# Cutting streamed weight loads by rows: 128 rows as one transfer, as 120+8, as 108+20 and as 63+63+2

## The chip, the cores and the metric

The kernel runs on one core of a Trainium2 chip. The metric is the device time of one execution in microseconds (us). Beside plain timed runs there is one profiled execution, whose trace holds every instruction, the semaphore updates and every DMA packet (queue, start, duration, size, but not the DMA engine that carried it). TensorE is PE here (PEld is its weight load), VectorE is DVE, ScalarE is ACT, GpSimd is POOL and SyncE is SP; a small q behind a name means the engine's instruction queue.

## The reference

Two attention mixers read the same 2048 x 640 input and are blended by a gate. Mixer A is what matters here: it goes through 64 segments of 32 tokens one after the other, because each segment hands 8 memory rows to the next.

```python
for s in range(n_seg):                       # 64 segments of 32 tokens
    xs = x[:, s * seg_len:(s + 1) * seg_len, :].copy()
    h = jnp.concatenate([mem, xs], axis=1)   # 8 memory rows + 32 tokens
    q = jnp.einsum('btd,dhe->bhte', h, Wq)   # 640 -> 32 heads x 192
    k = jnp.einsum('btd,dhe->bhte', h, Wk)
    v = jnp.einsum('btd,dhe->bhte', h, Wv)
    ...                                      # masked softmax attention over the 40 rows
    o = jnp.einsum('bhte,hed->btd', o, Wo)   # back to 640
    mem = o[:, :M, :].copy()
    outs.append(o[:, M:, :])
...
return g * a + (1 - g) * b                   # g = sigmoid(x . gate_w), b = local dilated attention
```

## The kernel before, in words

**Three stages.** Mixer B and the gate come first (`part_b`), then a pass over the last 8 tokens of all segments (`prepass`), then the loop over the 64 segments (`part_a`), and a short last stage (`part_z`). In the profiled execution the loop fills the time from about 360 to 1672 us.

**Weights.** The four weight matrices of mixer A are cut into 80 slices. A slice is 128 rows (partitions) of 3072 bytes, 384 KB. Most slices stay in SBUF for the whole loop. Fourteen of them (`N_STREAM`) do not fit and are fetched again from device memory in every segment. The list comes out of a small plan of due times in `weights_setup` (lines 510 to 534), which spreads the fourteen over the segment: seven for queries and keys, four for values, three for the output projection. The last three are read from a packed copy in device memory (`wscr`), the other eleven from the weight matrices themselves.

**The stream.** `get_slice` (line 576) gives a resident tile, or calls `load_slice`, which takes the next of five buffers (`WBUFS`, pool `wstream`, tiles `wst`) and issues one DMA from SP's queue (line 557 for the packed copy, line 558 for the matrices). SP's queue runs in order. A load can be issued as soon as PE has finished with the slice that was five places earlier in the stream, so it runs about five slices ahead of PE.

**Order of the work.** PE, ACT and DVE follow an order written out by hand in `part_a` (lines 907 to 986): projections `m_qk` (line 734), transposes `t_qk` (line 751), scores `s_a` and `s_b` (lines 781, 790), values `m_v` (line 827), the output projection `o_group` (line 891), and the selection `sel` (line 901) that makes the next segment's memory rows. ACT issues six small DMAs of its own in each segment: the result `out_dram` (line 1001), `Vz` (line 715), the next segment's tokens `hT` (line 650), a part of mixer B's result (line 954), `oz_dram` (line 968) and the next packed keys and queries `ZB` (line 710). They stand in ACT's order between its copies and exponentials.

**DMA semaphores.** All DMAs of SP and ACT share eight completion semaphores, taken in turn. In the trace each DMA waits, before it is issued, until the transfer that last used its semaphore has landed.

Of the kernel before, what the change touches and what calls it, by code (L numbers as in the profile page):

```python
# [27 lines left out]
class _K:  # L28
# [481 lines left out]
    def weights_setup(self):  # L510
        nc, tc = self.nc, self.tc
        keys = self.slice_keys()
        gap = {("q", 0, 0): 300, ("k", 0, 1): 160, ("k", 0, 3): 70, ("k", 1, 0): 450, ("k", 2, 0): 850, ("k", 3, 0): 1050,
               ("v", 1, 0): 1000, ("v", 2, 0): 600, ("v", 3, 0): 570, ("v", 3, 3): 200, ("oa", 6): 1200}
        at, t = {}, 0
        for k in keys:
            t += gap.get(k, 0)
            at[k] = t
            t += 163
        self.stream_keys = set()  # L520
        for i in range(N_STREAM):
            left = [k for k in keys if k not in self.stream_keys]
            self.stream_keys.add(min(left, key=lambda k: abs(at[k] - (i + 0.5) * t / N_STREAM)))
        rest = [k for k in keys if k not in self.stream_keys]
        use = [(m, R) for m in "qkv" for R in range(4)]
        rest.sort(key=lambda k: use.index(k[:2]) if k[:2] in use else 99)
        n = (0, N_EARLY, -N_MID - N_V - N_LAST, -N_V - N_LAST, -N_LAST, None)
        self.early, *self.late = [rest[n[x]:n[x + 1]] for x in range(5)]
        self.wres = self.ctx.enter_context(tc.tile_pool(name="wres", bufs=1))
        self.res_tiles = {}  # L530
        self.wscr = {}
        self.ahead = {}
        self.after = mybir.DependencyInfo(mybir.DependencyClass.Sync, mybir.DependencyReason.DATA)
        self.wstream = self.ctx.enter_context(tc.tile_pool(name="wstream", bufs=WBUFS))

# [13 lines left out]
    def load_slice(self, pool, key, name, tag=None, t=None):  # L549
        src = self.slice_info(key)[0]  # L550
        if t is None:
            t = pool.tile([128, 1536], BF, name=name, **({"tag": tag} if tag else {}))
            self.load_slice(pool, key, name, tag, t)
            return self.slice_view(key, t)
        v = self.slice_view(key, t)
        if key in self.wscr:
            return self.nc.sync.dma_start(t[:], self.wscr[key])
        return self.nc.sync.dma_start(v[:], src)

    def slice_view(self, key, t):  # L560
        split = self.slice_info(key)[1]
# [122 lines left out]
    def part_a(self):  # L684
# [4 lines left out]
        with ctx:  # L689
# [30 lines left out]

            sched = ctx.enter_context(tc.manual_schedule(engines={mybir.EngineType.PE, mybir.EngineType.Activation, mybir.EngineType.DVE}))
            for s in range(nseg):
                pqs, sts, pTs, pSs = {}, {}, {}, {}

                def m_qk(i, kcs):
# [391 lines left out]
```

## Time and profile before

| | before |
|---|---|
| median of two timed runs | 1725.18 us (1721.58 to 1728.78) |
| profiled execution, its own time | 1731.97 us |
| profiled execution, span from first to last instruction | 1729.2 us |
| PE busy | 1636.4 us, 95% of the span |
| DMA bytes over the span | 477.46 MB, mean 276 GB/s |
| streamed loads `wst` issued by SP | 260 + 260 + 195 + 192 of 384 KB |
| granted TensorE clock, mean | 0.990 |

PE's busy time is an upper bound of its useful time, since matmuls overlap in the pipeline and their ends are modelled. The mean share of the DMA engines adds up the durations of packets, and a packet that waits on its engine behind another queue's packet is counted too, so that the share can go above 1.

### The profile page before, as it was taken

The numbers are of one execution on the slowest core, as the hardware profiler recorded it, in microseconds if no ns is written. First come the engines' busy times: TensorE is split into PE (matmuls) and PEld (weight loads), VectorE is DVE, ScalarE is ACT, GpSimd is POOL, SyncE is SP. The second block draws the span as 40 slices with busy tenths as digits, with TensorE's granted clock in tenths as the row PEclk, the third lists the DMA queues.
The fourth block names the chain that finished last, engine by engine and source line by source line (L and its number), as shares of the span: only waits on it lengthen the run. The fifth ranks groups of instructions, "written<-read, shape, count | busy, mean of one in ns | idle before, by whom it ended". The sixth has DMA issues, their size and how long they took to land.

```text
span 1729.2 us, 82024 instructions
## 1 busy us (share of the span) xinstructions
PE 1636.4 (95%) x36281; PEld 976.2 (56%) x36281; DVE 632.3 (37%) x2031; ACT 861.4 (50%) x2338; POOL 59.8 (3%) x124
## 2 busy tenths in 40 slices
PE   7887999899999999999999999999999999999989
PEld 4544544355555655555555555556555556555667
DVE  3665333233333333333333333333333333333330
ACT  3887322235555555555555455555555545555550
POOL 2030000000000000000000000000000000000000
PEclk9999899999999999999999999999999999999999
DMA  7898695989999999899888889989899999998991
GB/s 198 202 228 199 226 319 146 273 276 298 294 301 301 299 299 308 294 294 305 298 291 298 281 290 302 301 292 306 299 297 301 297 290 303 305 300 298 310 295 31
DMA packets 299696, 477.46 MB, mean 276 GB/s; under 512 B 100172, under 2 KB 176460, under 8 KB 299340
## 3 DMA queue, kind: packets, MB, share of 16 engines
q1 hardware_dynamic: 200208, 415.76, 74.2%
q10 hardware_dynamic: 99132, 56.46, 11.5%
q8 instruction: 283, 4.64, 1.1%
q14 instruction: 73, 0.60, 0.1%
HBM read 430.40 MB, written 44.48 MB: 275 GB/s over the span
## 4 chain that ended last, share of the span: by engine, by line
PE 85%; DMA 6%; ACT 3%; issue 3%; DVE 1%; ACTq 1%; SPq 1%; DVEq 0%
PE ps_qk L734 25%; PE ps_v L827 13%; PE ps_wo L891 12%; PE ps_pre L603 6%; PE ps_qkT L751 6%; PE ps_S L781 5%; PE ps_oT L850 3%; PE ps_z L1048 3%; PE ps_pre L617 3%; ACT ZB L975 2%; DMA bqkT<-bqk_dram 2%; PE ps_bqk L234 2%; PE ps_mem L901 1%; PE ps_S L790 1%; DMA OT<-bo_dram 1%
## 5 line engine op out<-in xcount | busy, mean ns | idle before, releaser
L743 ACT CAST TZ<-ps_qk 128x384 bf16<-128x384 f32 x448 | 208.3, 479 | 333.5 <-PE ps_qk L734 189.3
L734 PEld LDWEIGHTS <-hT 128*32 128x32 bf16 x10240 | 247.0, 96 | 158.7 <-issue 17.2
L758 DVE COPY ZB<-ps_qkT 128x384 bf16<-128x384 bf16 x256 | 91.6, 358 | 376.8 <-PE ps_qkT L751 210.5
L734 PE MATMUL ps_qk<-wres_q,hT 128*32 128x384 bf16 x4096 | 225.2, 327 | 2.1 <-issue 2.1
L827 PE MATMUL ps_v<-wlate_v,hT 128*32 128x384 bf16 x4096 | 224.0, 328 | 0.0
L734 PE MATMUL ps_qk<-wlate_k,hT 128*32 128x384 bf16 x3328 | 202.7, 328 | 1.8 <-issue 1.8
L891 PEld LDWEIGHTS <-TZ 128*32 128x32 bf16 x6144 | 154.8, 96 | 68.6 <-issue 20.2
L734 PE MATMUL ps_qk<-wst,hT 128*32 128x384 bf16 x1792 | 154.0, 328 | 1.8 <-issue 1.1
L827 PEld LDWEIGHTS <-hT 128*32 128x32 bf16 x5120 | 113.4, 96 | 67.1 <-issue 4.3
L891 PE MATMUL ps_wo<-wlate_oa,TZ 128*32 128x384 bf16 x2560 | 140.1, 327 | 2.9 <-issue 2.2
L781 PE MATMUL ps_S<-ZB,TZ 128*128 128x160 bf16 (+1 forms) x1024 | 136.4, 237 | 0.3 <-DMA ZB<-zpk_dram 0.3
L891 PE MATMUL ps_wo<-wlate_ob,TZ 128*32 128x256 bf16 x2688 | 124.0, 275 | 8.4 <-issue 7.2
L751 PE MATMUL ps_qkT<-ident,TZ 128*128 128x128 bf16 x1536 | 129.7, 220 | 0.4 <-ACT TZ L743 0.3
L751 PEld LDWEIGHTS <-TZ 128*128 128x128 bf16 x1536 | 89.0, 98 | 61.2 <-issue 40.6
L799 ACT ACTIVATE ZB<-ps_S 32x224 bf16<-32x224 f32 x256 | 89.0, 348 | 42.6 <-PE ps_S L790 38.6
L861 DVE CAST TZ<-ps_oT 128x192 bf16<-128x192 f32 x256 | 79.5, 351 | 63.7 <-PE ps_oT L855 63.5
L861 ACT CAST TZ<-ps_oT 128x192 bf16<-128x192 f32 x256 | 69.8, 327 | 58.3 <-PE ps_oT L855 58.3
L781 PEld LDWEIGHTS <-TZ 128*128 128x128 bf16 (+1 forms) x1024 | 58.8, 95 | 67.8 <-issue 40.4
L904 DVE CAST hT<-ps_mem 128x24 bf16<-128x24 f32 x126 | 22.5, 179 | 202.3 <-PE ps_mem L901 202.3
L834 ACT CAST TZ<-ps_v 128x384 bf16<-128x384 f32 x192 | 92.4, 481 | 3.2
L827 PE MATMUL ps_v<-wst,hT 128*32 128x384 bf16 x1024 | 86.7, 329 | 3.6 <-DMA wst<-in_A_Wv_dram 3.6
L799 ACT ACTIVATE TZ<-ps_S 32x224 bf16<-32x224 f32 x256 | 88.8, 347 | 2.3
(137 smaller groups left out, 2229.9 us busy)
## 6 DMA issues: line engine op xcount, KB each, us to landing
wst<-in_A_Wq_dram SPq DMA_DIRECT2D x260, 384.0 KB
wst<-in_A_Wv_dram SPq DMA_DIRECT2D x260, 384.0 KB
wst<-in_A_Wk_dram SPq DMA_DIRECT2D x195, 384.0 KB
wst<-wscr SPq DMA_DIRECT2D x192, 384.0 KB
zpk_dram<-ZS ACTq DMA_DIRECT2D x4, 3072.0 KB
ZB<-zpk_dram ACTq DMA_DIRECT2D x64, 192.0 KB
wres_q<-in_A_Wq_dram SPq DMA_DIRECT2D x16, 384.0 KB
wlate_v<-in_A_Wv_dram SPq DMA_DIRECT2D x16, 384.0 KB
```

The source lines that it names most:

```text
L603: nc.tensor.matmul(ps[:], lhsT=sls[r][kc][:, c0:c0 + 128], rhs=zTi[:, kc, :], start=(kc == 0), stop=(kc == KC - 1))
L617: mm = nc.tensor.matmul(pss[g][:], lhsT=zTi[:, kc, 128 * st:128 * st + 128], rhs=sls[kc][:, 512 * g:512 * g + 512], start=(kc == 0), stop= ...
L734: nc.tensor.matmul(pq[32 * j:32 * j + 32, 0:384], lhsT=hT[:, kc, :], rhs=sl[:, 384 * j:384 * j + 384], start=(kc == 0), stop=(kc == KC - 1 ...
L743: cp(sts[i], pqs[i][:, 0:384])
L751: nc.tensor.transpose(pT[:, t, :, :, :].rearrange("p j b i -> p (j b i)"), st[:, 128 * t:128 * t + 128], self.ident[:])
L758: nc.vector.tensor_copy(q_blocks(R)[:, 1:5, :, :].rearrange("p b c i -> p c b i"), pT.rearrange("p t j b i -> p (t j) b i"))
L781: nc.tensor.matmul(grid(h, par)[:, :, 0:80].rearrange("p j (b r i) -> p j b r i", r=2, i=8)[:, :, :, r, :], lhsT=KT[k0:k1, 12 * r + c:12 * ...
L799: nc.scalar.activation(E[ps], pSs[h][ps, :, 112 * j:112 * j + 112], ACT.Exp, scale=scale_a)
L827: nc.tensor.matmul(pvs[R][32 * j:32 * j + 32, 0:384], lhsT=hT[:, kc, :], rhs=sl[:, 384 * j:384 * j + 384], start=(kc == 0), stop=(kc == KC ...
L834: cp(V[R], pvs[R][:, 0:384])
L861: cps[j % 2](oTxs[2 * h + j // 2][:, 6 * (j % 2):6 * (j % 2) + 6, :], pos[j][:, 0:240].rearrange("p (c q) -> p c q", q=40)[:, :, 8:40])
L891: nc.tensor.matmul(pso[part][32 * jj:32 * jj + 32, 0:n], lhsT=oTxs[2 * (R // 2) + j // 2][:, 6 * (j % 2) + 3 * (R % 2) + t, :], rhs=o_weig ...
```

## The change

A streamed slice is no longer always one DMA of 128 rows. A tuple `self.rows` lists row ranges, and `load_slice` issues one DMA from SP's queue for each range, into the same tile. The loop sets the tuple at the start of each segment: segments 0 to 9 and 58 to 63 keep one range of 128 rows; segments 10 to 25 use 120 and 8 rows; 26 to 41 use 108 and 20; 42 to 57 use 63, 63 and 2. The bytes are the same, and so are the buffers, the order of use and all arithmetic.

```diff
@@ weights_setup
         self.ahead = {}
+        self.rows = ((0, 128),)
         self.after = mybir.DependencyInfo(mybir.DependencyClass.Sync, mybir.DependencyReason.DATA)
@@ load_slice
         v = self.slice_view(key, t)
-        if key in self.wscr:
-            return self.nc.sync.dma_start(t[:], self.wscr[key])
-        return self.nc.sync.dma_start(v[:], src)
+        dst, src = (t, self.wscr[key]) if key in self.wscr else (v, src)
+        for r0, r1 in self.rows:
+            dma = self.nc.sync.dma_start(dst[r0:r1], src[r0:r1])
+        return dma
@@ part_a
             for s in range(nseg):
+                self.rows = (((0, 120), (120, 128)) if 10 <= s < 26 else ((0, 108), (108, 128)) if 26 <= s < 42 else
+                             ((0, 63), (63, 126), (126, 128)) if 42 <= s < 58 else ((0, 128),))
                 pqs, sts, pTs, pSs = {}, {}, {}, {}
```

## The prediction

> **What bounds the kernel now.** I read the page first (busy shares, the 40 slices, the DMA queues), then the stretches of the three groups of segments, who waited there, and last the trace's DMA packets and landings.
>
> ```profile
> PE   7887999899999999999999999999999999999989
> ...
> DMA  7898695989999999899888889989899999998991
> ...
> q1 hardware_dynamic: 200208, 415.76, 74.2%
> q10 hardware_dynamic: 99132, 56.46, 11.5%
> ```
>
> PE is at nine tenths through the loop, and so are the DMA engines: SP's queue (q1, nearly all of it the weight stream) and ACT's queue (q10) share them.
>
> ```profile
> 565.10:891.50 326.40, 315.94 (x7888) 192.12 (x7888) 116.82 (x432) 169.49 (x513) 8.11 (x16) 1.00 0.91 299
> 891.50:1220.40 328.90, 316.37 (x7883) 191.56 (x7884) 117.06 (x432) 169.48 (x512) 8.11 (x16) 1.00 0.90 296
> 1220.40:1546.20 325.80, 317.57 (x7893) 191.54 (x7892) 116.72 (x432) 169.46 (x512) 8.11 (x16) 1.00 0.91 299
> ```
>
> The columns are start and end, length, PE, PEld, DVE, ACT and POOL busy time, clock, DMA share and GB/s. The borders are the ends of the L975 copy, one per segment, so the lines are segments 10 to 25, 26 to 41 and 42 to 57. A segment takes 20.40, 20.56 and 20.36 us (length over 16), 19.70 at best; PE is busy 19.8 of it.
>
> ```profile
> PE ps_wo L891 <- issue: 7.3, 14, 1.1
> PE ps_qk L734 <- issue: 7.0, 8, 1.4
> PE ps_oT L850 <- issue: 3.5, 7, 0.9
> ```
>
> These are PE's longest waits in those 981 us. None is for a streamed slice: PE is the bound, and the stream keeps up. By how much is read from the packets. From 400 to 1640 us the trace has 108,758 stream packets of 3072 bytes, one per row: median 121 ns, mean 146.5. A load lands 4.4 to 4.7 us (median) after its issue; its buffer is needed 6.2 to 7.6 us after it. The slack is about two microseconds.
>
> **How many DMA engines a transfer uses.** The trace shows it by its landings. A 128-row load leaves 16 semaphore events, one per engine. The loads and stores of 20 rows in mixer B leave 11 (10 engines and one more from the queue itself, at once), the 8-row stores 9, the two small transfers of line 954 and line 1001, whose outer dimension is 4, leave 5. The largest divisor of the row count up to 16 fits all of these. It gives 15 engines for 120 rows, 12 for 108, 9 for 63 and 2 for 2.
>
> ```profile
> L250 SPq DMA_DIRECT2D bqkT<-bqk_dram x40: 273/358/1122, 24.3 to 169.4; - x40
> ```
>
> ```profile
> 168.40:171.00 2.60, 2.54 (x39) 1.15 (x32) 1.44 (x3) 2.15 (x4) 0.00 (x0) 0.52 0.54 105
> ```
>
> The first line are the 20-row loads (duration of the issue, min/median/max). Four are issued back to back into one tile, with no wait between them, so parts of one tile don't wait for each other. The second line is a stretch in which eight of them were in flight: a share of 0.54, under 10/16. In another, 28 to 29 us, 8 to 12 of their packets run at a time. So consecutive ones use the same ten engines and the others stand idle. I take it that every transfer begins at the same first engine.
>
> **The sum.** In rows per slice the busiest engine then carries 8 when whole, 8+1 = 9 with 120+8, 9+2 = 11 with 108+20, and 7+7+1 = 15 with 63+63+2. Fourteen slices make 112, 126, 154 and 210 packets per segment.
>
> That engine has other work in each segment. If the transfers on four engines lie on the same first ones, it is 2 x 32 packets of 320 bytes at 20 ns, 8 more for hT, 8 of 1536 bytes at 65, 16 of 768 at 36, and 20 completion packets at 9: 2.7 us, and 2.85 (two parts) or 3.0 (three) with the added completions. At the clean 121 ns the whole loads need 112 x 0.121 + 2.7 = 16.3 of 20.4 us, so the room is 4 us.
>
> What a packet costs in the parts no row shows directly. Below it can't be less than 121 ns, the undisturbed packet. Above, the nearest rows are mixer B's 20-row loads, whose 996-byte packets have medians of 69 to 92 ns in crowded stretches against 46 undisturbed, and the 3072-byte packets beside them 171 to 214 against 121: at most twice. The middle of that is 1.5 times, 181 ns. I take 146.5 ns, the mean in today's stream, because the 120-, 108- and 63-row parts are nearer to a whole load than to 20 rows.
>
> - 120+8: 126 x 0.1465 + 2.85 = 21.3 us, against 20.4: 0.9 more, over 16 segments **14 us**. (At 121: 18.1, nothing. At 181: 25.7, 84 us.)
> - 108+20: 154 x 0.1465 + 2.85 = 25.4, against 20.56: 4.85 more, **78 us**. (At 121: 15 us. At 181: 163.)
> - 63+63+2: 210 x 0.1465 + 3.0 = 33.8, against 20.36: 13.4 more, **214 us**. (At 121: 128. At 181: 330.)
>
> Together 306 us. Against the profiled execution's 1732 us (span 1729, three more around it) that is 2038; its time is 0.4% above the median of the runs, so **2030** is what I give. The ends are 1732 + 143 = 1875 and 1732 + 577 = 2309.
>
> [...]
>
> **Costs put at nothing.** The change adds 14 x 16 + 14 x 16 + 28 x 16 = 896 issues on SP at 0.33 us (the wst issues' median), 4.6 or 9.2 us per segment. They lie in SP's idle time: in these 981 us SP waited some 760 for PE.
>
> ```profile
> SPq L558 <- PE ps_qk L734: 256.2, 232, 3.0
> SPq L558 <- PE ps_wo L891: 132.2, 129, 2.4
> SPq L558 <- PE ps_v L827: 116.2, 96, 1.6
> ```
>
> Without that cover it is 42 issues x 0.37 = 15.5 us per segment in the third group, still under 20.4.
>
> The eight semaphores are the added wait. Twenty DMAs per segment become 34 and 48, and each waits for the eighth before it. Eight DMAs are then 3.3 or 2.3 slices instead of 5.6: the queue is at most that far ahead, which uses up the two microseconds of slack and brings nothing further where an engine is the bound anyway. Behind a waiting SP instruction stand only later slices. ACT is touched too: L1001 and L715 stand before the L743 copies, L954 before the exponential L799, L968 and L710 before the copies L975 and L983 on which PE's L901 and the next segment wait. Where SP lags, ACT's turn comes before its semaphore is free, and PE loses there, while the loads go on into free buffers. So I add nothing for it; it is one reason for staying above the clean ends.
>
> **Rivals.**
> [...]
> 2. *Clean packets.* Only the row counts decide, at 121 ns: 1875. For it: the median is 121 today, and part of the mean 146.5 is a packet's wait for ACT's queue, already in the 2.7 us. Against: a full queue never ran that clean.
> 3. *The eight semaphores alone.* Engines don't fill up, and a transfer lands 4.55 us after issue whatever its rows. Then a segment needs 34 x 4.55/8 = 19.3 us, nothing, or 48 x 4.55/8 = 27.3, 6.9 more: 1732 + 111 = 1843. Against: it leaves out the engines' load.
> 4. *Not slower.* The first engine changes from transfer to transfer, so the rows even out: 8 per engine on average, and a 63-row part lands sooner than a whole load (7 packets for 8). The 16.3 us stay 16.3 and the slack covers the rest: about 1732, within 25 us. It decides from the point where the busiest engine has under 20.4 us of work. Against: the ten packets at a time of the 20-row loads.
>
> **Chances.** My forecast 0.43; rival 1 0.22; rival 2 0.20; rival 3 0.06; rival 4 0.07; the rest, 0.02, is above all of these. The range 1860 to 2260 leaves out rivals 3 and 4 and the outer edges of the others, about 0.2. About 2% is what a measurement of this kernel can tell from no change. Slower by more: 0.93. Within it: 0.05, rival 4. Faster: 0.02, its lucky edge.
>
> **What would show it.** Cut at the L975 ends, segments 10 to 25 should take about 21 us, 26 to 41 about 25, 42 to 57 about 34, and the others 20.4. The DMA share should fall in this order while PE starts to wait for `DMA wst`. Landings per part should be 16 (15 and one), 9, 13, 11, 10, 10 and 3. [...] Landing counts other than these, or no waits of PE for `wst`, would make the whole argument wrong.

## The result, and the profile after

The changed kernel takes **2190.93 us** (median of two runs, 2185.70 to 2196.16) against 1725.18: 1.27 times as long, 95% interval 1.2527 to 1.2873. The profiled execution took 2185.7 us with a span of 2183.9, 454.7 more than before.

The page of the changed kernel: busy tenths and granted clock in 40 slices, then the DMA queues (packets, megabytes, share of 16 engines).

```profile
PE   8889999999887788778777877777767776777999
...
PEclk9998999999999999999989999998898888888999
DMA  7896888999888888887777777765555555556992
...
q1 hardware_dynamic: 204016, 415.78, 63.3%
q10 hardware_dynamic: 99132, 56.46, 9.9%
```

PE, at nine tenths through the whole loop before, is at seven to eight over the three groups and lowest in the last, where only half of the DMA engines' time is used. The bytes are the same; q1 has 3,808 packets more. These are completions: one per engine, 16 for a whole slice, and 15 + 8, 12 + 10 and 9 + 9 + 2 for the three cuts, so 224 x (7 + 6 + 4) = 3,808 more, to the packet. Now the three groups by themselves (start and end, length, PE, PEld, DVE, ACT, POOL busy, clock, DMA share, GB/s):

```profile
562.40:999.30 436.90, 349.49 (x7876) 195.00 (x7876) 117.59 (x432) 171.66 (x512) 8.15 (x16) 0.96 0.87 221
999.30:1441.20 441.90, 350.19 (x7888) 190.94 (x7888) 117.66 (x432) 171.52 (x512) 8.15 (x16) 0.97 0.73 220
1441.20:1998.10 556.90, 394.57 (x7896) 208.28 (x7898) 118.52 (x432) 172.66 (x513) 8.15 (x16) 0.87 0.54 176
```

Over 16 segments these are 27.3, 27.6 and 34.8 us per segment: 110, 113 and 231 us more than the same segments took before, 454 in all, which is the difference of the spans. What lies outside the groups moved by less than 3 us on either side.

PE's longest waits over the three groups (line, releaser: us in total, times, longest):

```profile
PE ps_qk L738 <- DMA wst<-in_A_Wq_dram: 99.2, 127, 3.8
PE ps_wo L895 <- DMA wst<-wscr: 86.7, 87, 3.0
PE ps_qk L738 <- DMA wst<-in_A_Wk_dram: 73.2, 92, 3.0
PE ps_v L831 <- DMA wst<-in_A_Wv_dram: 58.2, 81, 2.0
```

In these four lines PE waits 317 us for streamed slices; before, none of its longest waits was for one. Its own busy time grew too, by 144 us (1094 against 950) with the same matmuls. The two together are 461 us, about the difference. The granted clock, 1.00 before, was 0.96, 0.97 and 0.87. By itself that would make the busy time 4, 3 and 15% longer; it grew by 11, 11 and 24%, and what makes up the rest is open. A busy time that grows in this way is no sign that PE is the bound: the stretch with the most waiting has the lowest clock.

The first group differs from the other two in one more way: its DMA share is nearly that of before (0.87 against 0.91), and yet it moves 221 GB/s where 299 were moved. Its engines are hardly more idle; their packets take longer (188 ns for a weight packet on average, against 146.5). SP's queue in the first group:

```profile
SPq L559 <- DMA oz_dram<-TZ: 48.7, 13, 6.2
SPq L559 <- DMA wst<-in_A_Wv_dram: 44.4, 43, 2.0
SPq L559 <- DMA hT<-xh_dram: 43.5, 16, 4.4
SPq L559 <- DMA out_dram<-ZB: 28.8, 14, 3.5
SPq L559 <- DMA wst<-in_A_Wq_dram: 27.8, 21, 2.3
```

It used to wait for PE to free a buffer. Now it waits for landings, and three of these five are transfers that ACT issued: nothing but the shared completion semaphores ties them to SP.

### The profile page after: what moved, and what is told of

Same layout as the page of the kernel before. It is cut to its first block, busy times and chain, and to the rows that moved or that the text cites. A ratio compares the mean times of both kernels' runs of the same rounds, so it can differ in the third digit from the quotient of the medians.

```text
span 2183.9 us, 83257 instructions
## 1 busy us (share of the span) xinstructions
PE 1784.4 (82%) x36281; PEld 995.9 (46%) x36281; DVE 636.0 (29%) x2031; ACT 869.6 (40%) x2338; POOL 60.0 (3%) x124
## 4 chain that ended last, share of the span: by engine, by line
DMA 54%; PE 37%; SPq 3%; issue 2%; ACT 2%; DVE 1%; ACTq 1%; DVEq 0%
DMA wst<-in_A_Wq_dram 12%; DMA wst<-in_A_Wv_dram 10%; DMA wst<-wscr 9%; PE ps_qk L738 9%; DMA wst<-in_A_Wk_dram 6%; PE ps_pre L605 5%; PE ps_wo L895 5%; DMA out_dram<-ZB 4%; PE ps_v L831 4%; DMA ZB<-bsc_dram 4%; DMA ZB<-zpk_dram 3%; PE ps_z L1052 2%; PE ps_qkT L755 2%; PE ps_pre L619 2%; SPq L559 2%
## 5 line engine op out<-in xcount | busy, mean ns | idle before, releaser
L738 PEld LDWEIGHTS <-hT 128*32 128x32 bf16 x10240 | 252.7, 99 | 398.4 <-DMA wst<-in_A_Wq_dram 105.4
L738 PE MATMUL ps_qk<-wst,hT 128*32 128x384 bf16 x1792 | 161.3, 346 | 175.9 <-DMA wst<-in_A_Wq_dram 99.2
L738 PE MATMUL ps_qk<-wres_q,hT 128*32 128x384 bf16 x4096 | 237.6, 341 | 0.6 <-issue 0.6
L831 PE MATMUL ps_v<-wlate_v,hT 128*32 128x384 bf16 x4096 | 237.1, 343 | 0.0
L738 PE MATMUL ps_qk<-wlate_k,hT 128*32 128x384 bf16 x3328 | 211.4, 337 | 1.6 <-issue 1.6
L831 PEld LDWEIGHTS <-hT 128*32 128x32 bf16 x5120 | 121.1, 98 | 162.2 <-DMA wst<-in_A_Wv_dram 82.7
L895 PE MATMUL ps_wo<-wst,TZ 128*32 128x384 bf16 (+1 forms) x896 | 77.2, 333 | 94.9 <-DMA wst<-wscr 86.7
L895 PE MATMUL ps_wo<-wlate_oa,TZ 128*32 128x384 bf16 x2560 | 150.0, 345 | 1.7 <-issue 1.1
L831 PE MATMUL ps_v<-wst,hT 128*32 128x384 bf16 x1024 | 91.9, 348 | 63.1 <-DMA wst<-in_A_Wv_dram 61.9
L895 PE MATMUL ps_wo<-wlate_ob,TZ 128*32 128x256 bf16 x2688 | 137.0, 296 | 4.9 <-issue 4.9
L818 ACT ACTIVATE ps_S<-ps_S 128x160 f32<-128x160 f32 x128 | 38.1, 297 | 164.2 <-PE ps_S L815 160.8
```

The source lines that it names most:

```text
L738: nc.tensor.matmul(pq[32 * j:32 * j + 32, 0:384], lhsT=hT[:, kc, :], rhs=sl[:, 384 * j:384 * j + 384], start=(kc == 0), stop=(kc == KC - 1 ...
L831: nc.tensor.matmul(pvs[R][32 * j:32 * j + 32, 0:384], lhsT=hT[:, kc, :], rhs=sl[:, 384 * j:384 * j + 384], start=(kc == 0), stop=(kc == KC ...
L895: nc.tensor.matmul(pso[part][32 * jj:32 * jj + 32, 0:n], lhsT=oTxs[2 * (R // 2) + j // 2][:, 6 * (j % 2) + 3 * (R % 2) + t, :], rhs=o_weig ...
```

## The experiments

Three theories could each make a row-cut load late. **E**: the first engines carry more rows than the last ones, and the busiest sets the time. **S**: a packet of a cut load takes longer than one of a whole load. **T**: 34 or 48 transfers per segment take turns on eight semaphores, and each must wait for the landing of the eighth before it. All kernels below keep three groups of 16 segments. Each was profiled and timed once, beside a run of the kernel before on its chip (1725 to 1733 us). Diffs show the main lines only (`...` stands for lines left out), and the text says what each is against.

### Cutting by columns: neither E nor S

Against the kernel before:

```diff
-        return self.nc.sync.dma_start(v[:], src)
...
+        for c0, c1 in self.cols:
+            dma = self.nc.sync.dma_start(dst[:, c0:c1], src[:, c0:c1])
+        return dma
```

> A slice is cut by columns, all 128 rows in each part: two parts of 768 columns in segments 10 to 25, three of 512 in 26 to 41, whole in 42 to 57. The number of transfers, of issues on SP and of turns of the eight semaphores is that of the changed kernel (34 and 48 DMAs per segment, then 20), but each engine keeps an even share (16 packets of 1536 bytes at about 65 ns, or 24 of 1024 at about 46, per slice: 17 to 18.5 us of engine work per segment). Theory E (the busiest DMA engine is the bound): 20.4 us per segment in all three groups, about 1732 us in all. Theory S (the number of transfers is the bound, through the eight semaphores and through SP's queue, which now waits on landings of ACT's transfers): 27.3, 34.8 and 20.4 us per segment, about 2070 us.

1815.5 us; the segments take **20.8**, **25.4** and 20.3 us. The packets keep their price: 75.5 ns on average for half a row, 52.9 for a third, 147.7 for a whole one. So 34 transfers per segment cost 0.4 us as long as each has all 128 rows and all engines; the 6.9 us of the 120+8 group are not the number of transfers by itself. The 25.4 us of three parts lie between the two expectations (20.4 and 34.8). They looked like T at first. SP's own issues in those 406 us say otherwise (times issued, duration of an issue min/median/max in ns, first and last):

```profile
L561 SPq DMA_DIRECT2D wst<-in_A_Wv_dram x192: 327/430/1705, 904.6 to 1291.0; - x192
L561 SPq DMA_DIRECT2D wst<-in_A_Wq_dram x186: 327/430/2398, 896.5 to 1282.6; - x186
```

Their mean is 0.49 us, and 41.7 issues per segment make 20.4 of its 25.4 us; gaps above half a microsecond between them are 1.6 per segment, and short ones the rest. SP's issuing is the bound there. In the 63+63+2 group an issue takes 0.28 us on average, 11.9 of 34.8 us.

### Other row counts: E's rule, and where it falls short

Four kernels change only the row ranges: 112+16, 64+64, 96+32 in the first (whose diff is shown), 126+2, 117+11, 104+24 in the second, 63+65, 48+48+32, 60+60+8 in the third, and later, as a test of the rule far from the others, 124+4, 88+40, 100+28. Against the changed kernel:

```diff
-                self.rows = (((0, 120), (120, 128)) if 10 <= s < 26 else ((0, 108), (108, 128)) if 26 <= s < 42 else
-                             ((0, 63), (63, 126), (126, 128)) if 42 <= s < 58 else ((0, 128),))
+                self.rows = ((0, 112), (112, 128)) if 10 <= s < 26 else ((0, 64), (64, 128)) if 26 <= s < 42 else ((0, 96), (96, 128)) if 42 <= s < 58 else ((0, 128),)
```

> Cut by rows into parts that all run on 16 engines: 112+16 in segments 10 to 25, 64+64 in 26 to 41, 96+32 in 42 to 57; two transfers per slice, eight rows per engine in all. Theory S: 27.3 us per segment in all three groups, about 2068 us. Theory E without any sharing of ways into SBUF: 20.4 in all three, about 1732. [...]

> Two transfers per slice with ten rows on the busiest engine in all three groups: 126+2 rows (14 engines of nine rows, then two of one) in segments 10 to 25, 117+11 (13 of nine, 11 of one) in 26 to 41, 104+24 (13 of eight, 12 of two) in 42 to 57. Theory S: 27.3 in all three, about 2068 us. [...] Theory E with packets that are only crowded and not shared: 23 to 29 alike in all three.

> 63+65 rows in segments 10 to 25 (two transfers, 9 engines of seven rows, then 13 of five: twelve on the busiest), 48+48+32 in 26 to 41 (three transfers, all on 16 engines, eight rows on each), 60+60+8 in 42 to 57 (three transfers, 15, 15 and 8 engines, nine on the busiest). Theory E: 168 x 0.1445 + 2.85 = 27.1 us per segment in the first, 20.4 (no sharing) to 24.1 (at 188 ns) in the second, 21.2 to 26.7 in the third; about 1840 to 2000. Theory S: 27.3, 34.8 and 34.8; about 2300.

> Two transfers per slice on SP. 124+4 rows in segments 10 to 25: by the largest divisor up to 16, four engines of 31 rows and then four of one, 32 on the busiest. 88+40 in 26 to 41: 11 engines of eight and ten of four, 12 on the busiest. 100+28 in 42 to 57: ten engines of ten and 14 of two, 12 on the busiest. Landings 5 and 5, 12 and 11, 11 and 15 events. Theory E: 448 x 0.121 to 0.1465 + 2.85 = 57 to 68 us per segment in the first, 168 x 0.155 + 2.85 = 28.9 in the other two; about 2590 to 2770. Theory T (34 transfers): 27 in all three, about 2050.

They took 2024.2, 2045.6, 2216.6 and 2591.8 us. In the table, "busiest" is the number of packets that the busiest engine has per segment (14 slices times its rows, if each transfer starts at the same first engine), and "sum" is busiest x measured mean packet + 2.85 us (3.0 for three parts, 2.7 whole), the prediction's formula with the measured price in it. The price comes from the same stretch as the time, so an agreement shows that the parts fit together; it is no forecast.

| rows | landings per part | busiest | packet ns, mean (median) | sum, us | measured, us |
|---|---|---|---|---|---|
| 128, before | 16 | 112 | 146.5 (121) | 19.1 | 20.4 |
| **120+8** | 16, 9 | 126 | 188 (179) | 26.5 | 27.3 |
| **108+20** | 13, 11 | 154 | 158.6 (133) | 27.3 | 27.6 |
| **63+63+2** | 10, 10, 3 | 210 | 144.9 (121) | 33.4 | 34.8 |
| 112+16 | 16, 16 | 112 | 178.3 (158) | 22.8 | 26.1 |
| 64+64 | 16, 16 | 112 | 195.0 (194) | 24.7 | 27.4 |
| 96+32 | 16, 16 | 112 | 179.6 (164) | 23.0 | 26.2 |
| 126+2 | 15, 3 | 140 | 166.4 (134) | 26.1 | 26.3 |
| 117+11 | 14, 12 | 140 | 159.9 (127) | 25.2 | 27.0 |
| 104+24 | 14, 13 | 140 | 171.7 (156) | 26.9 | 27.9 |
| 63+65 | 10, 14 | 168 | 155.6 (127) | 29.0 | 29.4 |
| 48+48+32 | 16, 16, 16 | 112 | 175.9 (135) | 22.7 | 31.2 |
| 60+60+8 | 16, 16, 9 | 126 | 171.3 (126) | 24.6 | 31.1 |
| 124+4 | 5, 5 | 448 | 125.6 (124) | 59.1 | 56.7 |
| 88+40 | 12, 11 | 168 | 156.4 (132) | 29.1 | 29.6 |
| 100+28 | 11, 15 | 168 | 157.2 (131) | 29.3 | 28.7 |

The sum is good to about 2 us and no better: at 124+4 and 100+28 it is above the measured time, so what stands above it elsewhere is uncertain by as much.

Every landing count is the largest divisor of the rows up to 16, plus one from the queue where it is under 16. The strongest single line is 124+4, with four engines:

```profile
563.10:1470.80 907.70, 565.77 (x7876) 255.88 (x7876) 119.89 (x432) 177.06 (x512) 8.15 (x16) 0.55 0.29 107
```

The DMA share is 0.29, q1 has exactly four packets in flight for 80% of the stretch, and the segments take what 448 packets on one engine cost. Had the 4-row part run on other engines than the 124-row part, five to eight would run for much of the time; five or more did for 9%. The landings agree with the largest divisor of the row count up to 16, for all row counts of the table, and the four packets in flight with the same engines each time; which engines they are the trace does not say.

Two things are beyond E. First, cuts that load all engines evenly with eight rows, where E alone expects no loss, cost 6 to 7 us at two parts: their packets take 178 to 195 ns. Second, with even or nearly even engines the segment still stands about 3 us above the sum at 34 transfers and 6.5 to 8.5 above it at 48. The first is S. The second may be T or SP's issuing, which takes 18.3 of the 31.2 us at 48+48+32. Both needed kernels of their own.

### Packet times by themselves

These load whole slices, 20 transfers per segment as before, so neither T nor (for the first) E can act. Eleven of the fourteen slices come from padded copies in device memory, whose gaps cut the load into blocks of n neighbouring rows.

The copies are filled once, before the loop. The first kernel has 16 blocks of eight rows, each with a ninth row left empty behind it; against the kernel before:

```diff
+        scp = self.dram.tile([len(sp), 16, 9, 1536], BF, name="wpad")
...
+            self.pad[k] = scp[i, :, 0:8, :]
...
+        if self.blk and key in self.pad:
+            src = self.pad[key]
...
         return self.nc.sync.dma_start(v[:], src)
```

> Every slice is one whole transfer of 128 rows, 20 transfers per segment in all, but eleven of the fourteen slices come from a copy in device memory with a gap after every eight rows. In segments 10 to 25 its outer dimension is 16 (16 engines, eight neighbouring rows each), in 26 to 41 it is 8 (8 engines of 16 rows), in 42 to 57 the weights are read as before. Landings should be 16, 9 and 16 events. Theory T: 20.4 us per segment in the first and third group, and in the second 20 x 5.5 / 6 = 18, so 20.4 too; about 1735 to 1760 us. Theory E: second group 200 x 0.121 to 0.1465 + 2.7 = 26.9 to 32 us, first group 20.4, or 22.8 if neighbouring blocks of eight share ways into SBUF (188 ns), third 20.4; about 1840 to 1960.

> Whole transfers again, 20 per segment. The eleven slices of queries, keys and values come from padded copies in device memory, in blocks of 1 row (segments 10 to 25), 4 rows (26 to 41) and 16 rows (42 to 57); the three slices of the output projection stay as they were. Theory N (an engine that carries neighbouring rows shares its way into SBUF with others; the source plays no part): blocks of 1 row are as today, 20.4 us per segment at a mean of 147 ns (median 121); blocks of 4 lie between today and the blocks of eight, 20.4 to 23.1, at 121 to 182 ns; blocks of 16 leave 8 engines (9 landings) with 16 rows each, 11 x 16 + 3 x 8 = 200 packets at 121 to 182 ns: 27 to 39 us. Theory P (it was the padded source that made the packets of the eight-row blocks slow): blocks of 1 row are slow too, 23.1 us at 182 ns, and blocks of 4 the same.

The first took 1840.8 us, with blocks of eight in the first two groups (the second was meant to use eight engines; its landings were 16, so it repeats the first) and plain loads in the third. The second took 1924.8, with blocks of 1, 4 and 16. Their windows, columns as above:

```profile
585.40:956.30 370.90, 332.36 (x7888) 199.37 (x7888) 117.57 (x432) 170.72 (x513) 8.12 (x16) 0.98 0.99 262
956.30:1323.70 367.40, 328.16 (x7888) 196.61 (x7888) 117.46 (x432) 169.88 (x513) 8.11 (x16) 1.00 1.02 266
1323.70:1653.60 329.90, 317.55 (x7888) 191.85 (x7888) 116.83 (x432) 169.38 (x512) 8.12 (x16) 1.00 0.91 296
```

```profile
604.80:930.70 325.90, 316.26 (x7888) 191.34 (x7888) 116.79 (x432) 169.55 (x513) 8.15 (x16) 1.00 0.91 299
930.70:1256.70 326.00, 316.65 (x7883) 191.52 (x7884) 117.02 (x432) 169.68 (x513) 8.15 (x16) 1.00 0.91 297
1256.70:1739.00 482.30, 360.54 (x7893) 206.94 (x7892) 118.62 (x432) 173.95 (x512) 8.15 (x16) 0.93 0.63 203
```

- Blocks of eight: 23.2 and 23.0 us per segment, packets 182.4 and 183.8 ns (medians 182 and 185), all landings 16. The DMA share is 0.99 and 1.02 at 262 and 266 GB/s, where the plain loads have 0.91 at 296: engines that are occupied, not idle. So slow packets alone, S, cost **2.6 us** per segment.
- Blocks of 1 and of 4: 20.4 us, packets 147.3 and 147.6 ns (median 121). The padded source is not the cause.
- Blocks of 16: landings 9, so eight engines, 16 rows each, 200 packets on the busiest: 30.1 us, at 148.6 ns (median 124; the sum says 32.4). E without S. PE waits 117 us for slices there.

The sum for blocks of eight, 112 x 0.182 + 2.7 = 23.1, comes out too, but the engines are not simply the bound. SP waits there mostly for PE to free a buffer (449 us in both groups, against some 155 for landings), and PE's longest waits in the first group are these:

```profile
PE ps_wo L904 <- issue: 7.5, 6, 2.2
PE ps_oT L868 <- issue: 6.4, 4, 2.1
PE ps_qk L747 <- issue: 5.8, 4, 2.1
PE ps_v L840 <- DMA wst<-wpad: 4.9, 13, 0.8
```

Against the same segments before, both groups are 83 us longer: 28 in PE's busy time, 55 in its idle time. Only about 24 are waits for slices. 33 us lie in 25 stops of over 0.9 us in which neither PE nor PEld works and that no landing ends; each of them ends 1.3 to 2.1 us after a 16 KB packet of the queue q8, which the page calls "instruction", has landed. In the 48 segments before there were 7 such stops, 8 us in all. So it may be that PE's instructions come late too when the engines are full of slow packets; no run tested this.

What differs between these loads in the program is how their rows are cut, and no run shows why that sets the price. By median it is 121 ns for whole loads, for blocks of 1 and 4 and for 63+63+2, 124 for blocks of 16, 182 for blocks of 8 and 194 for 64+64. That engines share a way into SBUF, as Theory N has it, is not shown: the trace does not name the row of a packet. A rival is also left: with the blocks, the places in device memory that the engines read at the same time change too, and no run separates the reading from the writing.

One more kernel cut only some of the slices (seven 120+8, four 120+8, seven 63+65); against the kernel before:

```diff
-        return self.nc.sync.dma_start(v[:], src)
...
+        for r0, r1 in self.rows if key in self.some else ((0, 128),):
+            dma = self.nc.sync.dma_start(dst[r0:r1], src[r0:r1])
+        return dma
```

> Only some of the fourteen slices are cut: seven of them in 120+8 in segments 10 to 25 (27 transfers per segment), four in 120+8 in 26 to 41 (24 transfers), seven in 63+65 in 42 to 57 (27 transfers). Theory T: 27 x 4.9 / 6.2 = 21.3, 24 x 4.7 / 6.2 = 18.2 and 27 x 5.2 / 6.2 = 22.6 us, so 21.3, 20.4 and 22.6 us per segment, about 1785. Theory E (119, 116 and 140 rows on the busiest engine, packets of 167, 160 and 151 ns): 22.7, 21.4 and 23.9, about 1840. If the loss were in proportion to the number of cut slices: 23.9, 22.4 and 24.9.

1930.1 us; 25.4, 22.4 and 26.0 us per segment, above what both theories expected; of the three values in proportion to the cuts, only the 22.4 came true. The packets averaged 194, 173 and 176 ns over cut and whole loads together. The 194 with half of the slices cut is no less than the 188 with all of them cut, so it seems that a whole load that runs beside a cut one pays too; the trace does not tell their packets apart. With these prices the sums are 25.9, 22.9 and 27.4.

### The turns by themselves

Here the first part of a slice stays on SP and the others go out on POOL, so that SP and ACT have 20 transfers per segment again. POOL's copy into `KTz` moves to DVE to clear its queue. Against the changed kernel:

```diff
-            dma = self.nc.sync.dma_start(dst[r0:r1], src[r0:r1])
+            dma = (self.nc.gpsimd if r0 else self.nc.sync).dma_start(dst[r0:r1], src[r0:r1])
```

> The second part of each cut slice is issued from POOL's queue, so that SP and ACT together have 20 transfers per segment on their eight semaphores again, as before the change: 112+16 rows in segments 10 to 25, 120+8 in 26 to 41, 108+20 in 42 to 57. The copy of the packed keys moves from POOL to DVE so that POOL's queue is free. Theory T (each transfer waits for the eighth before it, about six are in flight, and a segment lasts as long as number of transfers x time to landing / 6): 20 x 5 / 6 = 16.7 us, so PE is the bound again, 20.4 to 21.5 us per segment in all three, about 1740 us. Theory E (the busiest DMA engine, with the packet times that these cuts showed: 178, 188 and 158 ns): 22.8, 26.5 and 27.2 us, about 1970.

> Three parts per slice, the second and third issued from POOL's queue, so that SP and ACT have 20 transfers per segment on their eight semaphores: 48+48+32 rows in segments 10 to 25, 60+60+8 in 26 to 41, 63+63+2 in 42 to 57 (the packed keys are copied by DVE instead of POOL). With all parts on SP these took 31.2, 31.1 and 34.8 us per segment. Theory E (the busiest engine, packets as slow as such cuts showed): 112 x 0.176 + 3 = 22.7, 126 x 0.171 + 3 = 24.6 and 210 x 0.145 + 3 = 33.4 us; the third less, down to 28, if POOL's parts use more engines than SP's (7 + 4 + 1 rows). About 1990, or 1900. Theory T alone: 20.4 to 21 in all three, about 1745. If neither the semaphores nor SP's queue matter: as with all parts on SP, about 2240.

| rows | all on SP, us | first part SP, rest POOL, us | difference |
|---|---|---|---|
| 112+16 | 26.1 | 23.7 | 2.4 |
| 120+8 | 27.3 | 25.8 | 1.5 |
| 108+20 | 27.6 | 26.5 | 1.1 |
| 48+48+32 | 31.2 | 24.6 | 6.6 |
| 60+60+8 | 31.1 | 24.1 | 7.0 |
| 63+63+2 | 34.8 | 27.3 | 7.5 |

(1964.2 and 1968.3 us.) For 112+16 the rest is the engines' sum, 112 x 0.1863 + 2.85 = 23.7. This is no proof that the engines are the bound, since PE waits only some 7 us for slices in that group and SP mostly for PE, as with the blocks of eight. So turns and SP's issuing together cost up to 2.4 us at 34 transfers and about 7 at 48 where the engines are even; these kernels do not separate the two. The last line must not be read so: POOL's transfers leave 16 landings whatever their rows, so they may not use the same engines, and there E is relieved as well. The same holds in a smaller way for 120+8 and 108+20, whose 1.5 and 1.1 are upper bounds.

The same with columns (three parts, two on POOL; two, one on POOL; four, all on SP) did not separate anything. Against the kernel before:

```diff
+        for c0, c1 in self.cols:
+            dma = (self.nc.gpsimd if c0 and self.pool else self.nc.sync).dma_start(dst[:, c0:c1], src[:, c0:c1])
```

> Cut by columns, all 128 rows in each part: three parts of 512 columns in segments 10 to 25 with the second and third issued from POOL, two of 768 in 26 to 41 with the second from POOL, four of 384, all from SP, in 42 to 57 (62 transfers per segment on the eight semaphores). Theory T: 20.4 to 21 us in the first (25.4 with all three on SP), 20.4 in the second, 62 x 3 / 6 = 31 in the third; about 1910 us. Theory E: engine work 15.5 to 18.5 us in all three, so 20.4 in all, about 1735. If a cut by itself costs through PE's or ACT's waits: 25 in the first again.

2124.1 us; 32.7, 22.4 and 30.7 us per segment. The first two are worse than the same cuts on SP (25.4 and 20.8). In the first group POOL's issues take 239 of 523 us (0.54 each); 170 more are idle time for which the profile shows no reason, and 76 are waits for the landings of slices. Why POOL is slow there is open: two or three parts in a row start 0.6 us apart, and 28 parts at that pace would take 17 us. The third is SP again: 55.3 issues at 0.488 us are 27.0 of 30.7, and its gaps above half a microsecond are 0.2.

Last, whole loads with 1, 2 or 4 added transfers of two rows of 32 bytes behind each, next to no work for the engines. Against the kernel before:

```diff
+        dma = self.nc.sync.dma_start(dst[:], src)
+        for _ in range(self.more):
...
+            self.nc.sync.dma_start(self.tiny[r:r + 2, :], self.Wq[r:r + 2, 0:16])
```

> Whole loads as before, and behind each of them 1 (segments 10 to 25), 2 (26 to 41) or 4 (42 to 57) added transfers of two rows of 32 bytes into a scratch tile: 34, 48 and 76 transfers per segment, with next to no work for the engines. Theory T (the turns of the eight semaphores cost what 34 and 48 transfers took away): at 4.55 us per landing 19.3, 27.3 and 43 us of turns, or with 2 us for the small ones 15, 18 and 25: 20.4, 20.4 to 27.3 and 25 to 43 us per segment, and SP waits for landings. Theory I (SP's own issuing is what counts, at 0.25 to 0.49 us each): 34 and 48 stay at 20.4, because 14 x 0.35 + 28 x 0.25 is 12 us; 76 takes 20.4 to 23, and SP's waits for landings stay small.

1975.2 us. The added transfers wait for nothing and so stood earlier in SP's queue than meant: 31 SP transfers per segment (37 with ACT's six) up to segment 50, and 70 (76) in segments 52 to 56. So the expectations for 34 and 48 were not tested. The stretches are segments 10 to 41, 42 to 50 and 52 to 56:

```profile
623.20:1326.90 703.70, 646.15 (x15776) 388.93 (x15776) 233.84 (x864) 338.20 (x1025) 16.23 (x32) 0.98 0.88 277
1326.90:1522.10 195.20, 180.27 (x4425) 108.42 (x4426) 65.69 (x243) 94.67 (x288) 4.56 (x9) 0.99 0.88 277
1558.60:1748.80 190.20, 132.70 (x2469) 73.08 (x2472) 36.72 (x135) 54.83 (x160) 2.54 (x5) 0.78 0.58 161
```

37 transfers: 703.7/32 = 22.0 us per segment, 1.6 more than with 20, where both theories gave 20.4 for 34. The stream is not late here. PE waits under 5 us for slices in these 32 segments; its longest waits are for ACT, and for DVE behind ACT:

```profile
PE ps_S L817 <- DVE ZB L810: 15.2, 11, 2.7
PE ps_mem L908 <- ACT ZB L982: 11.8, 17, 2.3
PE ps_qk L741 <- ACT TZ L750: 11.8, 11, 1.7
```

ACT itself waits some 70 us for landings, most of all for `wst` slices before its L750 copies (18.4 us). This fits the path that the prediction described under the eight semaphores: ACT's turn comes while its semaphore is taken, its copies stand behind that, and PE loses.

76 transfers: 190.2/5 = **38.0 us**, with DMA engines busy 58%, no packet of SP's queue in flight for a quarter of the time, and slice packets at 121 ns by median (175 by mean). SP's issues are 19.1 us of it (70 at 0.273); its waits there:

```profile
SPq L563 <- DMA wst<-in_A_Wv_dram: 12.1, 14, 2.2
SPq L559 <- DMA oz_dram<-TZ: 11.7, 4, 3.6
SPq L563 <- DMA wst<-in_A_Wq_dram: 11.5, 18, 2.1
SPq L563 <- DMA hT<-xh_dram: 11.3, 5, 3.3
SPq L563 <- DMA out_dram<-ZB: 11.1, 5, 2.7
```

All waits for landings are 75 us, 15 per segment. The theory of SP's issuing alone (20.4 to 23) fails, and T's range holds. A semaphore's round is 38.0 x 8/76 = 4.0 us: 2.5 from the start of an issue to its landing, and 1.4 in which it is free but the next transfer in turn is not issued yet. So half of the 38.0 us is SP's issuing and 15 its waits for landings: it is the two together that bind.

No version beat the kernel before.

## Why the prediction was right, and where it was off

The time, 2190.9, lies in the range (1860 to 2260), and "slower" had 0.93. The figure given, 2030, is 7% under it. Step by step:

- **Engines per transfer: right.** 16, 9, 13, 11, 10, 10 and 3 landings. That the transfers begin at the same engine each time 124+4 showed most plainly, with four packets in flight for 80% of its stretch.
- **Rows on the busiest engine: right, but of little weight in the first group.** 126, 154 and 210 packets with the measured prices give 26.5, 27.3 and 33.4 us of 27.3, 27.6 and 34.8. But 112+16, with even rows, took 26.1 us too, so in the first group the uneven rows add only about 1.2 of the 6.9 us. The falling DMA share (0.87, 0.73, 0.54) and PE's waits for `wst` came as said.
- **The packet's price: the mis-sized term.** The prediction took 146.5 ns for all three, "because the 120-, 108- and 63-row parts are nearer to a whole load than to 20 rows". Measured were 188, 158.6 and 144.9. The first group's extra 41.5 ns on 126 packets are 5.2 us per segment, 84 us in all, where 14 were forecast for the whole group; the second's 12 ns on 154 are 30 us; the third's are -5. Together 109 of the 148 us that the sum of 2038 was short of the profiled 2185.7. The upper bound, 181, was slightly too low for the first group. "At most twice", from which it came, was itself too low a reading: between 99 and 105 us of the run before, the 99 weight packets beside the 20-row loads have a median of 285 ns, 2.4 times 121. The order was wrong too (the first group costs nearly as much as the second, 110 and 113 us, where 14 and 78 were forecast): nearness to 128 rows says nothing, since 120 rows cost more than 63. That the total still came within 7% (2038 against 2185.7) is owed to the third group, which carried 214 of the 306 us and was right to 17. Luck has a part in it: the one price taken for all parts happened to fit this group.
- **The eight semaphores at nothing: slightly low.** What stands above the engines' sums is 0.8, 0.3 and 1.4 us per segment, some 40 us in all. This is within the sum's own error of 2 us; but the trace has stretches of the same size in which SP's queue has no packet in flight at all, 0.6, 0.2 and 1.7 us per segment (under 0.05 before). Moving the second part to POOL gave back at most 1.5 (120+8) and 1.1 (108+20). Turns and issuing would cost more if the engines did not hide them: about 7 us at 48 transfers with even engines. One argument fell short: the prediction followed the shared semaphores to ACT's waits, but three of SP's five longest waits in the first group are for ACT's transfers. The path through ACT itself showed only with the added small transfers, at 37 per segment.
- **SP's issues: right here.** 9.4 to 11.9 us per segment, beside waits for landings of 16 to 21. In the column cuts an issue took 0.49 us, and the cover was gone.

Slower packets there are, for a reason that no run shows: blocks of eight rows at unchanged transfers take 182 ns, 1.5 times 121, and the 108-row cut has them too (133 by median). Of the rivals, that of clean packets fits the 63-row median (121) and nothing else. The semaphore rival's 27.3 us for 48 transfers is not what bound the third group, and 48+48+32, at 31.2 against a sum of 22.7, is no clean case for it, since SP's issues are 18.3 of that. The even-rows rival is excluded by the packets in flight: 13 or fewer for 99% of the second group, 10 or fewer for 99% of the third, where 14 or more ran for half of the time before.

## What to carry to other kernels

For loads issued from SP, count the packets of the busiest DMA engine, not the bytes: at the same bytes, 112, 210 and 448 of them per segment took 20.4, 34.8 and 56.7 us here. The count that fits these runs is the rows divided by their largest divisor up to 16 (as the landings have it), added over the parts as if all began at the same engine (as the four packets in flight at 124+4 have it). The packet time has to be measured for the shape, since an even split, 64+64, cost a third more per packet (195 ns against 146.5 by mean). In these runs the cheapest cut was by columns, in two, with all 128 rows in each: 0.4 us per segment. Then count the transfers on the shared semaphores and SP's issues: 37 transfers in place of 20 cost 1.6 us per segment of 20.4, and 48 with even engines about 7. ACT's transfers on those semaphores delayed the stream (SP waited 121 us for three of them in the first group), and the stream's delayed ACT (some 70 us of waits for landings at 37 transfers).

## What was not expected of the hardware

- A part's packet time changes with the cut, at the same 3072 bytes: 121 ns (median) for whole loads and for blocks of 1 and 4 rows, 182 for blocks of 8, 194 for 64+64, 121 again for 63+63+2 with nine engines.
- An issue on SP is not one price: 0.28 us (mean) for 63- and 2-row parts, 0.34 for 120+8, 0.49 for 128 rows of a column cut, 0.60 for 64+64. POOL needs 0.54 for the issue of a 128-row part.
- POOL's transfers left 16 landings for 8 and even for 2 rows.
- The granted PE clock fell where PE waited: 1.00 in the loop before, 0.87 at 34.8 us per segment, 0.55 at 56.7, with busy times of 318, 395 and 566 us for the same matmuls. It does not follow the segment's length alone: 0.98 at 30.7 us (four column parts), 0.95 at 25.4 (three).
- In the run before and with blocks of eight rows, the longer stops of PE with no visible reason end 1.3 to 2.1 us after a 16 KB packet of the instruction queue has landed.
